# Late pieces of a second weight matrix: eight instead of six, in finer steps, and two groups' second layer moved into the third group

## The chip, the cores and the metric

The kernel runs on one core of one Trainium2 chip. What counts is device time in microseconds for one execution of the whole program. Three runs of the kernel before took 918.93, 920.24 and 922.5 us; their median is 920.24 us.

## The reference

Three layers follow each other: causal attention with a decay, a routed layer of experts of which each token uses one, and a dense two-layer network. The change lies in the weights of the last of them and touches the time around it.

```python
x = _moe_ref(x=attention_out, **moe_kwargs)      # 2304 tokens, 512 wide
...
def _moe2_ref(x, w_in, w_out, alpha):
    h = x @ w_in                                 # 512 -> 2048
    g = np.maximum(h, 0.0) + alpha * np.minimum(h, 0.0)
    return (g @ w_out).astype(np.float32)        # 2048 -> 512
```

The caller hands over `w_in` and `w_out` as 64-bit floats.

## The kernel before

Every matrix product is made of 16-bit halves: a number is held as a high half and the rest as a low half, and three matmuls (high by high, high by low, low by high) stand for one. The weights come from memory in 64 bits, so a piece of 128 rows by 512 columns is first turned to 32 bits on DVE by five bit operations (`ffn_bits`, L1445 to L1462) and then split (`ffn_split`, L1465): ACT writes the high half (L1474), DVE subtracts it for the low half (L1475). There are 32 pieces: 16 of `w_in` (tile `wi`) and 16 of `w_out` (tiles `wo` and, for the late ones, `wob`).

*The stage of token blocks.* Some 20 blocks of 128 gathered tokens go through their expert's two layers: `hidden` (L1186, 24 matmuls for both halves of a block, then ACT and DVE make the halves `hs`), `hturn` (L1209, SP transposes them by DMA into `ht`), and `outer` (L1221, 24 matmuls that read `ht`, then ACT and DVE write `yr`, and GpSimd scatters it to `ys`). The loop over `s` issues `hidden` and `hturn` of block `s + 1` ahead of `outer` of block `s`; blocks are called by these numbers below. Between them stand steps of a list `work`: 26 pieces of the dense weights (`KH + 16 - LATE`) and, one after every third piece, 8 parts of the third expert's weights. A step (`convert`, L1515) does the bits of one entry, the split of the entry before, and fetches the entry four later into one of four buffers. For an expert part the first half of a step is the high half on ACT and the second the low half on DVE (`part_hi`, `part_lo`, L1490 and L1495). The steps are dealt out evenly over the loop, half before and half after `outer`:

```python
    per = len(work) / (NS - NX - 0.5)
        due += per / 2
        while at_[1] < min(due, len(work)):
            convert()
        outer(s, wsel(s)[1])
```

With `NS` 20 and `NX` 7 the divisor is 12.5. A fetch is issued by SP, in the order of the program, and so are the transposes.

*The dense layers.* Tokens come in five groups: group 0 of 256, groups 1 to 4 of 512. `ffn_in(j, m)` makes one of 16 tiles of the first layer for group `j`: 12 matmuls into one of four PSUM buffers (L1668), two DVE operations that read it (L1673, L1676), the high half `g` on ACT (L1680), the low half on GpSimd (L1681). `ffn_out(j, t)` makes the output of 128 tokens: 48 matmuls over all 16 `g` tiles of its group (L1690), a copy on ACT, a scatter on GpSimd. The pool of `g` has 26 buffers. The outputs of group `j - 1` follow inside group `j`, in group 1 after tile 7, later after tile 3 (L1730).

The 6 pieces that are left (`LATE`) are converted here: `late_step` (L1706) is called once ahead of the loop and at seven tiles, and does the split of one piece, the bits of the next and the fetch of the one after it. The order of all engines' instructions is that of the program, from the token blocks on.

Of the kernel before, what the change touches and what calls it, by code (L numbers as in the profile page):

```python
# [11 lines left out]
F16 = mybir.dt.float16  # L12
# [73 lines left out]
SI = 32.0  # L86
SO = 64.0
# [4 lines left out]
def kernel(  # L92
# [19 lines left out]
    N, DM = out.shape  # L112
    E, _, F = w1.shape
    DFF = w_in.shape[1]
    P = 128
# [3 lines left out]
    KH = DFF // P  # L119
# [20 lines left out]
    G0 = 256  # L140
# [1272 lines left out]
    cvp = mid.enter_context(tc.tile_pool(name="cvp", bufs=2))  # L1413
    wst[0] = mid.enter_context(tc.tile_pool(name="wst3", bufs=4))
    with_w = ctx.enter_context(tc.tile_pool(name="wffn", bufs=1, side="right"))
    LATE = 6
    wi = with_w.tile([P, 2, KD, DFF], F16, name="wi")
    wo = [with_w.tile([P, 2, KH - LATE, DM], F16, name="wo")]
    x2a = with_w.tile([P, 2, KD, G0], F16, name="x2a")
# [42 lines left out]
        )  # L1462
        return tk

    def ffn_split(g, tk):  # L1465
        if g < 16:
            dk, cg = divmod(g, 4)
            cs_ = slice(cg * 512, cg * 512 + 512)
            dst, sc = wi, SI
        else:  # L1470
            y, dk = divmod(g - 16, KH - LATE)
            cs_ = slice(0, DM)
            dst, sc = wo[y], SO
        nc.scalar.activation(out=dst[:, 0, dk, cs_], in_=tk, func=AF.Copy, scale=sc)  # L1474
        nc.vector.scalar_tensor_tensor(  # L1475
            out=dst[:, 1, dk, cs_], in0=tk, scalar=sc, in1=dst[:, 0, dk, cs_], op0=ALU.mult, op1=ALU.subtract
        )


    ex2 = nc.sync.value_load(i8[0:1, 2:3], min_val=0, max_val=E - 1)  # L1480
# [18 lines left out]

    PS = (KH + 16 - LATE) // (KD + KF // 2)  # L1500
    work = []
    for g in range(KH + 16 - LATE):
        work.append((lambda g=g: ffn_fetch(g), lambda t, g=g: ffn_bits(g, t), lambda t, g=g: ffn_split(g, t)))
        if g % PS == 0 and g // PS < KD + KF // 2:
            y = g // PS
# [135 lines left out]
    gp = ctx.enter_context(tc.tile_pool(name="gp", bufs=26))  # L1641
# [9 lines left out]
    groups = [(0, G0)] + [(t, min(512, N - t)) for t in range(G0, N, 512)]  # L1651
# [10 lines left out]
    def ffn_in(j, m):  # L1662
        n = groups[j][1]
        x2 = x2s[j]
        hps = ps_a.tile([P, 512], F32, tag="a", name="a")
        for kk in range(KD):
            for y, (l, mm) in enumerate(((0, 0), (0, 1), (1, 0))):
                nc.tensor.matmul(  # L1668
                    hps[:, 0:n], lhsT=wi[:, mm, kk, m * P:(m + 1) * P], rhs=x2[:, l, kk, 0:n],
                    start=(kk == 0 and y == 0), stop=(kk == KD - 1 and y == 2),  # L1670
                )
        t = fp.tile([P, 512], F32, tag="t", name="t")
        nc.vector.tensor_scalar(  # L1673
            out=t[:, 0:n], in0=hps[:, 0:n], scalar1=0.0, scalar2=al[:, m:m + 1], op0=ALU.min, op1=ALU.mult
        )
        nc.vector.scalar_tensor_tensor(  # L1676
            out=t[:, 0:n], in0=hps[:, 0:n], scalar=0.0, in1=t[:, 0:n], op0=ALU.max, op1=ALU.add
        )
        g = gp.tile([P, 2, 512], F16, tag="g", name="g")
        nc.scalar.activation(out=g[:, 0, 0:n], in_=t[:, 0:n], func=AF.Copy)  # L1680
        nc.gpsimd.tensor_tensor(out=g[:, 1, 0:n], in0=t[:, 0:n], in1=g[:, 0, 0:n], op=ALU.subtract)  # L1681
        gts[j, m] = g

    def ffn_out(j, t):
        t0, n = groups[j]
        ops = ps_o.tile([P, DM], F32, tag="o", name="o")
        for m in range(KH):
            g = gts[j, m]
            for y, (l, mm) in enumerate(((0, 0), (0, 1), (1, 0))):
                nc.tensor.matmul(  # L1690
                    ops, lhsT=g[:, l, t * P:(t + 1) * P], rhs=wo[m // (KH - LATE)][:, mm, m % (KH - LATE), :],
                    start=(m == 0 and y == 0), stop=(m == KH - 1 and y == 2),
                )
        ob = fp.tile([P, DM], F32, tag="ob", name="ob")
        nc.scalar.activation(out=ob, in_=ops, func=AF.Copy, scale=1.0 / (SY * SI * SO))  # L1695
        ti = t0 // P + t
        nc.gpsimd.indirect_dma_start(  # L1697
            out=out[:, :], out_offset=IndirectOffsetOnAxis(ap=tka[:, ti:ti + 1], axis=0), in_=ob,
            in_offset=None, bounds_check=N - 1, oob_is_err=False,
        )  # L1700
# [2 lines left out]
    lraw = []  # L1703
    lbits = []

    def late_step():  # L1706
        if lbits:
            g, tk = lbits.pop(0)
            ffn_split(g, tk)
        if lraw:  # L1710
            g, raw = lraw.pop(0)
            lbits.append((g, ffn_bits(g, raw)))
        if late:
            g = late.pop(0)
            lraw.append((g, ffn_fetch(g)))

    x2s[0] = x2a
    order2 = ExitStack()
    order2.enter_context(tc.manual_schedule(engines=
# [3 lines left out]
    for j in range(len(groups)):  # L1723
        if j + 1 < len(groups):
            load_x2(j + 1)
        for m in range(KH):
            ffn_in(j, m)
            if (j, m) in ((0, 5), (0, 10), (0, 15), (1, 1), (1, 3), (1, 5), (1, 6)):
                late_step()
            if m == (7 if j == 1 else 3) and j > 0:  # L1730
                for t in range(groups[j - 1][1] // P):
                    ffn_out(j - 1, t)
    for t in range(groups[-1][1] // P):
        ffn_out(len(groups) - 1, t)
    order2.close()
# [30 lines left out]
```

## Time and profile before

| | us |
|---|---|
| median of three runs | 920.24 |
| profiled execution, its own time | 921.76 |
| its span, first to last instruction | 920.0 |
| TensorE busy | 802.4 (87%) |
| DVE busy | 503.6 (55%) |
| ACT busy | 320.8 (35%) |
| GpSimd busy | 287.1 (31%) |

The mean granted clock of TensorE is 0.950 of full speed. Busy time is an average over stages: the 87% holds stretches without a gap and stretches that wait, so the views by stretch and by time are the ones to read. Matmuls overlap, and the duration of one (379 ns) is longer than the distance between two. An idle time in square brackets is what the engine stood before that instruction, with what ended it.

### The profile page before, as it was taken

To read this page: it belongs to the slowest core of one execution; us is meant where nothing else is said; L and a number is where in the kernel's file an instruction comes from. 1 tells how busy PE (TensorE), PEld (TensorE's weight loads), DVE (VectorE), ACT (ScalarE), POOL (GpSimd) and SP (SyncE) were. 2 spreads that over 40 slices of the span, in tenths; PEclk is the share of its full clock that TensorE was granted. 3 is DMA by queue.
4 is the path that set the end of the run, shared out by engine and by line. 5 is a ranking of instruction groups with operands and counts; after the bars stand their busy time and mean duration, and the time that the engine had idled before them with its cause. 6 is when DMAs were issued, how large, how long until landed. Compare 5 with 4: busy or idle time off the path is not lost. (4 is left out here: it accounts for less than half of the span.)

```text
span 920.0 us, 15632 instructions
## 1 busy us (share of the span) xinstructions
PE 802.4 (87%) x5562; PEld 448.4 (49%) x5565; DVE 503.6 (55%) x1244; ACT 320.8 (35%) x630; POOL 287.1 (31%) x347
## 2 busy tenths in 40 slices
PE   3887759667988786989998899999999999999995
PEld 2676747554766332434443384444444444444442
DVE  6887859695785253668886768542035005302400
ACT  5786648574665122423232222121012002101200
POOL 4444344342435224421321133232034104302400
PEclk9998889887999897999999999999999999999998
DMA  7979999999852897999999354002002000000000
GB/s 151 167 134 183 160 130 175 183 195 167 133 77 60 137 145 193 257 267 223 244 233 240 92 120 114 12 12 58 24 12 46 12 35 1 1 24 23 1 24 23
DMA packets 226632, 103.17 MB, mean 112 GB/s; under 512 B 192843, under 2 KB 213944, under 8 KB 226554
## 3 DMA queue, kind: packets, MB, share of 16 engines
q1 hardware_dynamic: 221018, 87.29, 51.8%
q0 software_dynamic: 5536, 14.86, 4.7%
q8 instruction: 46, 0.75, 0.4%
q14 instruction: 32, 0.26, 0.1%
HBM read 49.06 MB, written 15.59 MB: 70 GB/s over the span
## 5 line engine op out<-in xcount | busy, mean ns | idle before, releaser
L1668 PE MATMUL a<-x,wi 128*128 128x512 f16 x768 | 168.2, 382 | 0.0
L1673 DVE TENSOR_SCALAR t<-a,al 128x512 f32<-128x512 f32 (+1 forms) x80 | 55.6, 695 | 203.7 <-PE a L1668 203.7
L1668 PEld LDWEIGHTS <-wi 128*128 128x128 f16 x960 | 95.2, 99 | 100.0 <-issue 7.5
L1690 PEld LDWEIGHTS <-g 128*128 128x128 f16 x864 | 84.5, 98 | 103.7 <-POOL g L1681 1.2
L1681 POOL TENSOR_TENSOR g<-t,g 128x512 f16<-128x512 f32 (+1 forms) x80 | 84.7, 1059 | 128.4 <-ACT g L1680 126.7
L1231 PE MATMUL y<-wcc,ht 128*128 (+1 forms) x456 | 108.3, 394 | 15.3 <-DMA ht<-hs 15.1
L1690 PE MATMUL o<-wo,g 128*128 128x512 f16 x540 | 119.5, 379 | 0.0
L1196 PE MATMUL h<-wcc,xgt 128*128 (+1 forms) x456 | 106.7, 390 | 11.3 <-DMA xgt<-xg 10.9
L1680 ACT ACTIVATE g<-t 128x512 f16<-128x512 f32 (+1 forms) x80 | 46.9, 587 | 163.9 <-DVE t L1676 163.9
L662 PE MATMUL pt<-identf,t 128*128 128x128 f32 x384 | 66.1, 298 | 32.3 <-DVE p L678 14.3
L650 ACT ACTIVATE t<-e,nm 128x512 f32<-128x512 f32 (+2 forms) x144 | 81.4, 603 | 18.5 <-DVE e L627 13.7
L1231 PEld LDWEIGHTS <-ht 128*128 128x128 f16 x480 | 47.7, 100 | 78.3 <-DMA ht<-hs 21.2
L1196 PEld LDWEIGHTS <-xgt 128*128 128x128 f16 x480 | 47.6, 100 | 69.5 <-DMA xgt<-xg 11.5
L678 DVE SCALAR_TENSOR_TENSOR p<-pt,p 128x512 f16<-128x512 f32 x96 | 65.4, 682 | 23.8 <-ACT p L671 23.3
L1690 PE MATMUL o<-wob,g 128*128 128x512 f16 x324 | 73.2, 379 | 1.5 <-DVE wob L1475 0.9
L1695 ACT ACTIVATE ob<-o 128x512 f32<-128x512 f32 x18 | 10.7, 596 | 158.2 <-PE o L1690 158.2
L627 DVE TENSOR_SCALAR_CACHE_REDUCE e<-s 128x512 f32<-128x512 f32 (+3 forms) x128 | 58.0, 480 | 13.1 <-PE s L580 13.1
L1697 POOL DMA_INDIRECT out_dram<-ob,tka x18 | 17.6, 978 | 151.3 <-ACT ob L1695 151.2
L662 PEld LDWEIGHTS pt<-identf,t 128*128 128x128 f32 x384 | 43.7, 150 | 36.2 <-ACT t L650 20.2
L671 ACT ACTIVATE p<-pt 128x512 f16<-128x512 f32 x96 | 56.2, 586 | 12.4 <-PE pt L662 12.1
L1676 DVE SCALAR_TENSOR_TENSOR t<-a,t 128x512 f32<-128x512 f32 (+1 forms) x80 | 51.0, 638 | 2.8
L579 PE MATMUL s<-yw,wcc 128*128 128x256 f16 (+1 forms) x192 | 47.4, 273 | 4.0 <-DMA yw<-wcc 4.0
(307 smaller groups left out, 1097.7 us busy)
## 6 DMA issues: line engine op xcount, KB each, us to landing
raw<-in_moe_w_in_dram SPq DMA_DIRECT2D x16, 512.0 KB, 7.1
raw<-in_moe_w_out_dram SPq DMA_DIRECT2D x16, 512.0 KB, 3.8
yw<-wcc SPq DMA_DIRECT2D x14, 320.0 KB, 5.0
kn<-in_k_dram SPq DMA_DIRECT2D x16, 256.0 KB, 4.3
qn<-in_q_dram SPq DMA_DIRECT2D x32, 128.0 KB, 4.4
vn<-in_v_dram SPq DMA_DIRECT2D x16, 256.0 KB, 4.0
xs<-nat SPq DMA_DIRECT2D x16, 256.0 KB, 7.1
ht<-hs SPq DMA_TRANSPOSE x40, 4.9
```

The lines of the kernel that those rows point to most:

```text
L627: nc.vector.tensor_scalar(out=e[:, c0:c0 + w], in0=ps[:, c0:c0 + w], scalar1=-1.0 / 8.0, scalar2=3.0e38, op0=ALU.mult, op1=ALU.min, accum_ ...
L650: nc.scalar.activation(out=natural(t[:, c0:c0 + w]), in_=halves(e[:, c0:c0 + w]), func=AF.Exp, scale=-1.0, bias=nm[:, y:y + 1])
L662: nc.tensor.transpose(pt[:, c * P:(c + 1) * P], e[:, c * P:(c + 1) * P], identf)
L671: nc.scalar.activation(out=p[:, 0, 0:512], in_=U[u][0], func=AF.Copy, scale=SP)
L678: nc.vector.scalar_tensor_tensor(out=p[:, 1, 0:512], in0=U[u][0], scalar=SP, in1=p[:, 0, 0:512], op0=ALU.mult, op1=ALU.subtract)
L1196: nc.tensor.matmul(hps, lhsT=xgt[:, kk, l, :], rhs=m1(m, kk, cs_), start=(kk == 0 and y == 0), stop=(kk == KD - 1 and y == 2),)
L1231: nc.tensor.matmul(yps, lhsT=ht[:, kk // (KF // 2), l, kk % (KF // 2), :], rhs=m2(m, kk), start=(kk == 0 and y == 0), stop=(kk == KF - 1 a ...
L1668: nc.tensor.matmul(hps[:, 0:n], lhsT=wi[:, mm, kk, m * P:(m + 1) * P], rhs=x2[:, l, kk, 0:n], start=(kk == 0 and y == 0), stop=(kk == KD - ...
L1673: nc.vector.tensor_scalar(out=t[:, 0:n], in0=hps[:, 0:n], scalar1=0.0, scalar2=al[:, m:m + 1], op0=ALU.min, op1=ALU.mult)
L1676: nc.vector.scalar_tensor_tensor(out=t[:, 0:n], in0=hps[:, 0:n], scalar=0.0, in1=t[:, 0:n], op0=ALU.max, op1=ALU.add)
L1681: nc.gpsimd.tensor_tensor(out=g[:, 1, 0:n], in0=t[:, 0:n], in1=g[:, 0, 0:n], op=ALU.subtract)
L1690: nc.tensor.matmul(ops, lhsT=g[:, l, t * P:(t + 1) * P], rhs=wo[m // (KH - LATE)][:, mm, m % (KH - LATE), :], start=(m == 0 and y == 0), s ...
```

## The change

`LATE` becomes 8, so that `wo` holds 8 pieces and `wob` 8, and the list `work` has 24 pieces and 8 parts. The late step is cut finer: the high half stands in one step and the low half in the next, so that a piece goes through four steps (fetch, bits, high half, low half), and within a step the low half of the oldest piece comes first. There are ten calls in the loop instead of seven, the last two in group 2. The outputs of groups 0 and 1 both come after tile 7 of group 2; group 0's `g` tiles get 16 smaller buffers of their own.

```diff
@@ -1413,7 +1413,7 @@
     cvp = mid.enter_context(tc.tile_pool(name="cvp", bufs=2))
     wst[0] = mid.enter_context(tc.tile_pool(name="wst3", bufs=4))
     with_w = ctx.enter_context(tc.tile_pool(name="wffn", bufs=1, side="right"))
-    LATE = 6
+    LATE = 8
     wi = with_w.tile([P, 2, KD, DFF], F16, name="wi")
     wo = [with_w.tile([P, 2, KH - LATE, DM], F16, name="wo")]
     x2a = with_w.tile([P, 2, KD, G0], F16, name="x2a")
@@ -1462,19 +1462,26 @@
         )
         return tk
 
-    def ffn_split(g, tk):
+    def ffn_place(g):
         if g < 16:
             dk, cg = divmod(g, 4)
-            cs_ = slice(cg * 512, cg * 512 + 512)
-            dst, sc = wi, SI
-        else:
-            y, dk = divmod(g - 16, KH - LATE)
-            cs_ = slice(0, DM)
-            dst, sc = wo[y], SO
+            return wi, SI, dk, slice(cg * 512, cg * 512 + 512)
+        y, dk = (0, g - 16) if g - 16 < KH - LATE else (1, g - 16 - (KH - LATE))
+        return wo[y], SO, dk, slice(0, DM)
+
+    def ffn_high(g, tk):
+        dst, sc, dk, cs_ = ffn_place(g)
         nc.scalar.activation(out=dst[:, 0, dk, cs_], in_=tk, func=AF.Copy, scale=sc)
+
+    def ffn_low(g, tk):
+        dst, sc, dk, cs_ = ffn_place(g)
         nc.vector.scalar_tensor_tensor(
             out=dst[:, 1, dk, cs_], in0=tk, scalar=sc, in1=dst[:, 0, dk, cs_], op0=ALU.mult, op1=ALU.subtract
         )
+
+    def ffn_split(g, tk):
+        ffn_high(g, tk)
+        ffn_low(g, tk)
 
 
     ex2 = nc.sync.value_load(i8[0:1, 2:3], min_val=0, max_val=E - 1)
@@ -1676,7 +1683,10 @@
         nc.vector.scalar_tensor_tensor(
             out=t[:, 0:n], in0=hps[:, 0:n], scalar=0.0, in1=t[:, 0:n], op0=ALU.max, op1=ALU.add
         )
-        g = gp.tile([P, 2, 512], F16, tag="g", name="g")
+        if j == 0:
+            g = gp.tile([P, 2, G0], F16, tag="g0", name="g0", bufs=KH)
+        else:
+            g = gp.tile([P, 2, 512], F16, tag="g", name="g")
         nc.scalar.activation(out=g[:, 0, 0:n], in_=t[:, 0:n], func=AF.Copy)
         nc.gpsimd.tensor_tensor(out=g[:, 1, 0:n], in0=t[:, 0:n], in1=g[:, 0, 0:n], op=ALU.subtract)
         gts[j, m] = g
@@ -1686,9 +1696,10 @@
         ops = ps_o.tile([P, DM], F32, tag="o", name="o")
         for m in range(KH):
             g = gts[j, m]
+            wm, mo = (wo[0], m) if m < KH - LATE else (wo[1], m - (KH - LATE))
             for y, (l, mm) in enumerate(((0, 0), (0, 1), (1, 0))):
                 nc.tensor.matmul(
-                    ops, lhsT=g[:, l, t * P:(t + 1) * P], rhs=wo[m // (KH - LATE)][:, mm, m % (KH - LATE), :],
+                    ops, lhsT=g[:, l, t * P:(t + 1) * P], rhs=wm[:, mm, mo, :],
                     start=(m == 0 and y == 0), stop=(m == KH - 1 and y == 2),
                 )
         ob = fp.tile([P, DM], F32, tag="ob", name="ob")
@@ -1703,10 +1714,16 @@
     lraw = []
     lbits = []
 
+    lhalf = []
+
     def late_step():
+
+        if lhalf:
+            ffn_low(*lhalf.pop(0))
         if lbits:
             g, tk = lbits.pop(0)
-            ffn_split(g, tk)
+            ffn_high(g, tk)
+            lhalf.append((g, tk))
         if lraw:
             g, raw = lraw.pop(0)
             lbits.append((g, ffn_bits(g, raw)))
@@ -1714,6 +1731,8 @@
             g = late.pop(0)
             lraw.append((g, ffn_fetch(g)))
 
+
+    LSTEPS = ((0, 5), (0, 11), (1, 0), (1, 3), (1, 6), (1, 9), (1, 12), (1, 15), (2, 2), (2, 5))
     x2s[0] = x2a
     order2 = ExitStack()
     order2.enter_context(tc.manual_schedule(engines=
@@ -1725,11 +1744,12 @@
             load_x2(j + 1)
         for m in range(KH):
             ffn_in(j, m)
-            if (j, m) in ((0, 5), (0, 10), (0, 15), (1, 1), (1, 3), (1, 5), (1, 6)):
+            if (j, m) in LSTEPS:
                 late_step()
-            if m == (7 if j == 1 else 3) and j > 0:
-                for t in range(groups[j - 1][1] // P):
-                    ffn_out(j - 1, t)
+            if m == (7 if j == 2 else 3) and j > 1:
+                for i in (0, 1) if j == 2 else (j - 1,):
+                    for t in range(groups[i][1] // P):
+                        ffn_out(i, t)
     for t in range(groups[-1][1] // P):
         ffn_out(len(groups) - 1, t)
     order2.close()
```

What moves on the engines is shown at three places. First DVE in group 0, around the second late step in the loop (`t` is a tile's result, `ta` and `tb` the bit tiles, `wob` the late weights); before, after tile 10:

```order
L1673 TENSOR_SCALAR t<-a,al 128x256
L1676 SCALAR_TENSOR_TENSOR t<-a,t 128x256
L1475 SCALAR_TENSOR_TENSOR wob<-ta,wob 128x512
L1451 TENSOR_SCALAR ta<-raw 128x512
L1452 TENSOR_SCALAR ta<-ta 128x512
L1454 TENSOR_SCALAR tb<-ta 128x512
L1457 SCALAR_TENSOR_TENSOR tb<-raw,tb 128x512
L1460 SCALAR_TENSOR_TENSOR ta<-raw,tb 128x512
L1673 TENSOR_SCALAR t<-a,al 128x256
L1676 SCALAR_TENSOR_TENSOR t<-a,t 128x256
```

and now, after tile 11:

```order
L1680 TENSOR_SCALAR t<-a,al 128x256
L1683 SCALAR_TENSOR_TENSOR t<-a,t 128x256
L1451 TENSOR_SCALAR ta<-raw 128x512
L1452 TENSOR_SCALAR ta<-ta 128x512
L1454 TENSOR_SCALAR tb<-ta 128x512
L1457 SCALAR_TENSOR_TENSOR tb<-raw,tb 128x512
L1460 SCALAR_TENSOR_TENSOR ta<-raw,tb 128x512
L1680 TENSOR_SCALAR t<-a,al 128x256
L1683 SCALAR_TENSOR_TENSOR t<-a,t 128x256
```

The low half left this step; the five bit operations stay, one tile later.

Next DVE in the token blocks, from the first conversion that follows `yr` of block 8 to `hs` of block 10. Before (the bits of the first conversion and `yr` stand just ahead):

```order
L1475 SCALAR_TENSOR_TENSOR wi<-ta,wi 128x512
L1451 TENSOR_SCALAR ta<-raw 128x512
L1452 TENSOR_SCALAR ta<-ta 128x512
L1454 TENSOR_SCALAR tb<-ta 128x512
L1457 SCALAR_TENSOR_TENSOR tb<-raw,tb 128x512
L1460 SCALAR_TENSOR_TENSOR ta<-raw,tb 128x512
L1475 SCALAR_TENSOR_TENSOR wi<-ta,wi 128x512
L1204 SCALAR_TENSOR_TENSOR hs<-h,hs 128x512 x2
```

and now, from `yr` of block 8:

```order
L1244 SCALAR_TENSOR_TENSOR yr<-y,gs,yr 128x512
L1451 TENSOR_SCALAR ta<-raw 128x512
L1452 TENSOR_SCALAR ta<-ta 128x512
L1454 TENSOR_SCALAR tb<-ta 128x512
L1457 SCALAR_TENSOR_TENSOR tb<-raw,tb 128x512
L1460 SCALAR_TENSOR_TENSOR ta<-raw,tb 128x512
L1478 SCALAR_TENSOR_TENSOR wi<-ta,wi 128x512
L1204 SCALAR_TENSOR_TENSOR hs<-h,hs 128x512 x2
```

One conversion of five bit operations and a low half left this stretch.

Last SP's queue in the dense layers, where `raw` is a late fetch and `x` a group's tokens. Before:

```order
L1440 DMA raw<-in_moe_w_out_dram 128x1024
L1423 DMA_TRANSPOSE x_7726<-ys 128x8x512
L1428 DMA tka<-ys 128x4x1
L1440 DMA raw<-in_moe_w_out_dram 128x1024 x3
L1423 DMA_TRANSPOSE x_8064<-ys 128x8x512
L1428 DMA tka<-ys 128x4x1
L1440 DMA raw<-in_moe_w_out_dram 128x1024 x2
L1423 DMA_TRANSPOSE x_8512<-ys 128x8x512
L1428 DMA tka<-ys 128x4x1
L1423 DMA_TRANSPOSE x_9035<-ys 128x8x512
L1428 DMA tka<-ys 128x4x1
```

and now:

```order
L1440 DMA raw<-in_moe_w_out_dram 128x1024
L1423 DMA_TRANSPOSE x_7704<-ys 128x8x512
L1428 DMA tka<-ys 128x4x1
L1440 DMA raw<-in_moe_w_out_dram 128x1024 x2
L1423 DMA_TRANSPOSE x_8030<-ys 128x8x512
L1428 DMA tka<-ys 128x4x1
L1440 DMA raw<-in_moe_w_out_dram 128x1024 x5
L1423 DMA_TRANSPOSE x_8401<-ys 128x8x512
L1428 DMA tka<-ys 128x4x1
L1423 DMA_TRANSPOSE x_9035<-ys 128x8x512
L1428 DMA tka<-ys 128x4x1
```

Group 2's tokens are loaded after two fetches in group 0 rather than three, and five fetches stand ahead of group 3's tokens.

## Rows read from the trace of the kernel before

**Rows 1.** Stretches, TensorE: start:end and length, busy (instructions), granted clock, DMA share, GB/s.

```profile
376.00:527.00 151.00, 139.06 (x632) 0.99 0.92 226
600.00:900.00 300.00, 300.00 (x1392) 1.00 0.07 21
```

**Rows 2.** TensorE's waits, 376 to 527 us: us in total, times, longest.

```profile
PE y L1231 <- DMA ht<-hs: 11.7, 7, 2.6
```

**Rows 3.** Order of time, TensorE, outer products: start, us, instruction, [idle before and releaser].

```profile
411.22 6.83 PE L1231 MATMUL y<-wcc,ht 128*128 x24 [2.58 <-DMA ht<-hs]
...
425.04 5.34 PE L1231 MATMUL y<-wcc,ht 128*128 x24 [1.82 <-DMA ht<-hs]
...
447.62 5.34 PE L1231 MATMUL y<-wcc,ht 128*128 x24 [1.70 <-DMA ht<-hs]
...
479.66 5.34 PE L1231 MATMUL y<-wcc,ht 128*128 x24 [0.62 <-DMA ht<-hs]
...
491.91 0.38 PE L1231 MATMUL y<-wcc,ht 128*128 x1 [1.73 <-DMA ht<-hs]
...
521.37 5.36 PE L1231 MATMUL y<-w2x,ht 128*128 128x512 f16 x24 [1.98 <-DMA ht<-hs]
```

**Rows 4.** Order of time, DVE and SP's queue around block 9's transposes.

```profile
402.60 1.22 DVE L1497 SCALAR_TENSOR_TENSOR w1x<-wst__6087,w1x 128x1024 f16<-128x1024 f32 x1
...
404.48 5.09 SPq L1217 DMA_TRANSPOSE ht<-hs  x2
```

**Rows 5.** Groups of DVE instructions, 376 to 527 us: busy, mean ns, idle before.

```profile
L1204 DVE SCALAR_TENSOR_TENSOR hs<-h,hs 128x512 f16<-128x512 f32 x26 | 17.2, 684 | 12.4 <-ACT hs L1203 12.4
...
L1475 DVE SCALAR_TENSOR_TENSOR wi<-ta,wi 128x512 f16<-128x512 f32 x16 | 10.9, 683 | 1.4 <-ACT wi L1474 1.4
...
L1244 DVE SCALAR_TENSOR_TENSOR yr<-y,gs,yr 128x512 f16<-128x512 f32 x13 | 9.7, 746 | 12.3 <-ACT yr L1243 12.3
```

**Rows 6.** Order of time, 530 to 620 us: around the late steps.

```profile
548.61 0.74 DVE L1475 SCALAR_TENSOR_TENSOR wob<-ta,wob 128x512 f16<-128x512 f32 x1 [1.00 <-ACT wob L1474]
549.27 0.42 DVE L1451 TENSOR_SCALAR ta<-raw 128x512 uint32<-128x512 uint32 x1
...
551.99 0.48 DVE L1673 TENSOR_SCALAR t<-a,al 128x256 f32<-128x256 f32 x1
...
552.84 0.47 DVE L1673 TENSOR_SCALAR t<-a,al 128x256 f32<-128x256 f32 x1
...
552.98 1.58 PE L1668 MATMUL a<-x2a,wi 128*128 128x256 f16 x12 [1.95 <-DVE t L1676]
...
560.70 0.74 DVE L1673 TENSOR_SCALAR t<-a,al 128x512 f32<-128x512 f32 x1
...
562.08 0.74 DVE L1673 TENSOR_SCALAR t<-a,al 128x512 f32<-128x512 f32 x1
...
562.86 0.69 DVE L1676 SCALAR_TENSOR_TENSOR t<-a,t 128x512 f32<-128x512 f32 x1
562.90 1.16 POOL L1681 TENSOR_TENSOR g<-t,g 128x512 f16<-128x512 f32 x1 [5.39 <-ACT g L1680]
...
587.17 0.38 PE L1690 MATMUL o<-wob,g 128*128 128x512 f16 x1 [0.61 <-ACT wob L1474]
...
588.43 0.59 PE L1690 MATMUL o<-wob,g 128*128 128x512 f16 x2 [0.88 <-DVE wob L1475]
```

**Rows 7.** Chain of work that ended last: start, us, engine.

```profile
599.38 31.08 PE a L1668 x144
```

**Rows 8.** Stretches of 4 us, TensorE, columns as in rows 1.

```profile
554.00:558.00 4.00, 4.00 (x15) 0.57 1.17 285
...
586.00:590.00 4.00, 2.51 (x12) 1.00 0.00 0
```

**Rows 9.** Instructions of the conversion tiles: ns least/median/most, first and last start.

```profile
L1454 DVE TENSOR_SCALAR tb<-ta x32: 426/427/778, 380.9 to 582.7; 128x512 uint32<-128x512 uint32 x32
...
L1475 DVE SCALAR_TENSOR_TENSOR wob<-ta,wob x6: 741/1224/1230, 548.6 to 587.1; 128x512 f16<-128x512 f32 x6
```

## The prediction

> **What bounds the kernel now.** I read the stretches of engine time first, then TensorE's waits, then the order of time around each wait.
>
> From 600 to 900 us TensorE is busy without a break at full clock [rows 1]. Nothing the change does there can save time, unless it opens a gap. From 376 to 527 us, the stage of token blocks, TensorE is busy for 139.06 of 151 us [rows 1], and its one named wait is for the transposed hidden block `ht`: 11.7 us in all [rows 2]. Two kinds of wait can be told apart in order of time [rows 3]. The outer products at 411.22, 447.62 and 479.66 (blocks 9, 12, 15) come after a half block whose last conversion step is an expert part. SP's next fetch then needs a buffer that only that part's low half frees, so the transposes queue behind it: the low half at 402.60, the transposes from 404.48 [rows 4]. Those at 425.04, 491.91 and 521.37 (blocks 10, 16, 19) come after a block with three bit conversions on DVE.
>
> Between 529 and 600 us lie three losses around the late pieces. DVE stands 1.00 us before the low half at 548.61, because it follows the high half in the same step, and then runs five bit operations (549.27 to 551.99); four PSUM buffers fill and TensorE stands 1.95 us [rows 6]. From 554 to 558 the granted clock is 0.57 [rows 8], a mix of the levels 1.2 and 2.4 GHz, so 4 x 0.43 = 1.72 us are lost. At 587 TensorE stands 0.61 and 0.88 us for the last late piece [rows 6]; the clock stays at 1.00 there [rows 8]. Sum: 1.95 + 1.72 + 1.49 = **5.16 us**.
>
> **The change, part by part.**
>
> *The second step of group 0* now holds only bits. Before, DVE gave TensorE nothing from about 547.5 (the end of its work on the eleventh tile) to 551.99, some 4.5 us. Now it is 2.72 us (549.27 to 551.99 [rows 6]), or 3.07 if one operation is stretched as the longest 778 ns against 427 [rows 9]. A group-0 tile takes TensorE 1.30 us (half of 31.08/12 = 2.59 [rows 7]), and three free buffers cover 3.9 us. DVE needs 0.85 us per tile there (551.99 to 552.84 [rows 6]), so the six tiles between steps give back 6 x 0.45 = 2.7 us. No stall; the 1.95 and the 1.72 go.
>
> *The steps in group 1* come every three tiles: DVE spends 3 x 1.38 (560.70 to 562.08 [rows 6]) + 2.72 bits + 0.68 low [rows 5] = 7.54 us against TensorE's 3 x 2.59 = 7.77. High halves run on ACT a step ahead, so the 1.00 us wait is gone. If the low half takes 1.23 and one bit operation 0.78 [rows 9], it is 8.44: 0.67 lag per step, 4.0 over six steps. The cover is three buffers, 7.77, less one step's 4.3: 3.5 us. So the worst by these rows is half a microsecond of stall, perhaps with one more 1.72 of clock, and I take none. Here the cover is nearly used up: if DVE is slower than that, its tiles are late next.
>
> *The two moved pieces* add to this stage two fetches, ten bit operations, two high and two low halves. The DVE part is in the sums above, the high halves go to ACT beside one operation per tile. SP now issues eight fetches; each waits for the bits of the piece two earlier, and behind the last five stands only group 3's load, which TensorE reads after the 62 us of output tiles.
>
> *Second layer later.* TensorE runs group 1 whole and half of group 2 (24 tiles, 24 x 2.59 = 62 us) before the first late piece is read; that is at about 552 + 62 + 24 matmuls x 0.216 = 619. The last low half comes after the sixth tile of group 2, at about 610. The 1.49 goes. Six output tiles in a row follow instead of two and four; matmuls and scatters are the same in number. The separate smaller buffers for group 0 hold its results longer: with 16 of group 1 and 8 of group 2, 24 of 26 buffers are in use. Cost nothing.
>
> *The stage of token blocks* loses two of 26 pieces: 2 x (2.72 + 0.68) = 6.8 us of DVE, and two fetches on SP. A block costs TensorE 48 matmuls of 0.216 (31.08/144 [rows 7]), 10.36 us. Three bit conversions in a block make DVE 3 x 2.72 + 2 x 0.68 + 1.22 [rows 4] + 0.75 + 2 x 0.68 [rows 5] = 12.9; with two it is 9.5. By the rule in the code, 34 steps become 32 over 12.5 blocks: three-bit blocks fall from four to two (blocks 13 and 16; hidden blocks 15 and 18 follow them), part-last half blocks from four to three (before blocks 9, 14, 17). Block 9 keeps its 2.58. For 14 and 17 I take the mean of 1.70 and 0.62, 1.16 each. Of the first three three-bit blocks two cost 1.82 and 1.73 and one nothing: 1.18 each for the two left. Block 19's 1.98 goes: between hs of 18 and of 19 DVE now has one bit conversion where it had three. The 1.3 us of 11.7 that lies outside the six rows I leave. Sum 2.58 + 2.32 + 2.36 + 1.3 = 8.5, a gain of **3.2 us**. Bounds: all waits but block 9's vanish (gain 9.1); the five marked blocks all wait 2.58, 12.9 in all (loss 1.2).
>
> Total 5.16 + 3.2 = 8.4 us. The profiled execution took 921.76, so 913.4; it lies 1.5 above the median of the runs, 920.24. Against the median: **911.9 us**.
>
> **The rivals.**
>
> *The waits in the token blocks only move* (TensorE, no longer late, meets the next transpose early). For: waits there also follow slow transposes, not DVE alone. Against: the three-bit blocks. 920.24 - 5.16 = 915.1.
>
> *The split does not do what it says:* in group 0 the bits are the stall, not the wait for ACT, and 1.95 + 1.72 stay. Against: 2.72 is below the cover of 3.9. 920.24 - 1.49 - 3.2 = 915.5.
>
> *Slower: GpSimd holds DVE up in group 1.* The wob low halves took 741 to 1230 ns [rows 9] where the same operation takes 683 [rows 5]; GpSimd's subtraction of g lasts 1.16 us [rows 6], once per tile, and the late steps now run amid it instead of after a wait. If each subtraction holds DVE for its whole length, three tiles cost 7.54 + 3 x 1.16 = 11.0 us against 7.77: 3.2 lag, 19.4 over six steps, less 3.5 cover: 15.9 of stall, with 1.72 of clock. 920.24 - 5.16 + 17.6 - 3.2 = 929.5. It decides from about 1.8 us of lag per step, where stall and clock eat the 8.4. Against: the stretch seen is 0.55 us, not 1.16, and the tile operation at 562.86 keeps its 0.69 with the subtraction at 562.90 beside it [rows 6]. The Trainium skill has this as a rule ("SBUF — State Buffer", section "Who interferes with whom"): a DVE instruction with two SBUF inputs and a GpSimd instruction that reads SBUF use one shared read interface, and the second to start waits for the whole of the first. By that rule it would come out as in this rival; the trace agrees that there is a hold-up, but with about half that size.
>
> **How the numbers follow.** Forecast 0.64, moving waits 0.22, split without effect 0.09, slower 0.05. A measurement of this kernel tells 0.5% from no change, 4.6 us: faster is below 915.6. The forecast counts as faster; the two cases near 915 count by a little over half (0.13 and 0.05): faster 0.82, same 0.13, slower 0.05. The range: from 906.5 (the gain of 9.1 nearly whole, with 5.16) to 917, which takes in both cases near 915 with half the bound of 1.2 and one half-microsecond stall with its clock.
>
> **What would show it.** Right: no TensorE wait for `t` or `wob`, no clock below 1.00 between 535 and 600, DVE without waits for ACT at wob's low half, the six output tiles in one block of 62 us, and `ht` waits near 8.5 us with none at block 10 or 19. Wrong: a TensorE wait for `t` in group 1 or 2, low halves over 1.23 us, or `ht` waits of 11 us or more.

## The result, and the profile after

The changed kernel took 909.13 us (median of four runs, 903.85 to 917.96), the kernel before 919.59 on the same chip (four runs, 918.5 to 922.5). The ratio is 0.989, with an interval of 0.985 to 0.993: faster by 6.8 to 13.6 us. Ratios and intervals, here and below, leave out executions in the chip's second, slower state, so a ratio is not quite that of the two medians. The forecast was 911.9, 8.3 us below the kernel before. The total came out near; two of its terms did not, and they erred in opposite directions.

The page's first lines of the changed kernel, the share of each engine (its profiled execution took 907.73 us):

```profile
span 905.6 us, 15603 instructions
## 1 busy us (share of the span) xinstructions
PE 796.8 (88%) x5565; PEld 446.1 (49%) x5565; DVE 511.5 (56%) x1244; ACT 320.6 (35%) x630; POOL 291.5 (32%) x347
```

DVE is busy for 7.9 us more than the 503.6 before (4.4 more in the repetition below), though the same pieces are converted. That is the first sign that some operations became longer. TensorE's waits from 360 us to the end of the changed kernel (total, times, longest):

```profile
PE y L1231 <- DMA ht<-hs: 6.8, 2, 3.8
PE a L1675 <- DVEq L1564: 2.8, 1, 2.8
PE a L1675 <- DVE t L1683: 2.7, 4, 1.0
```

The waits for `ht` fell from 11.7 us in 7 to 6.8 in 2 [rows 2]. The waits for `wob` are gone. The wait of 2.8 ahead of the dense layers is as it was. The waits for `t`, which were to go, are four now. In order of time on TensorE, the places of these waits in the token blocks and group 0's start:

```profile
407.44 7.03 PE L1231 MATMUL y<-wcc,ht 128*128 x24 [3.82 <-DMA ht<-hs]
...
495.41 5.35 PE L1231 MATMUL y<-wcc,ht 128*128 x24 [2.99 <-DMA ht<-hs]
...
510.96 5.34 PE L1231 MATMUL y<-w2x,ht 128*128 128x512 f16 x24
...
519.13 11.08 PE L1675 MATMUL a<-x2a,wi 128*128 128x256 f16 x100 [2.83 <-DVEq L1564]
```

Only blocks 9 (407.44) and 17 (495.41) wait, both after a half block that ends with an expert part; block 14, the third such, does not. Block 19 (510.96) waits for nothing, where it stood 1.98 us [rows 3]. The dense layers of the changed kernel, TensorE, DVE and GpSimd in order of time:

```profile
540.67 36.42 PE L1675 MATMUL a<-x,wi 128*128 128x512 f16 x168 [0.42 <-DVE t L1683]
...
553.35 1.15 DVE L1478 SCALAR_TENSOR_TENSOR wob<-ta,wob 128x512 f16<-128x512 f32 x1
...
561.63 0.69 DVE L1683 SCALAR_TENSOR_TENSOR t<-a,t 128x512 f32<-128x512 f32 x1
561.68 1.16 POOL L1691 TENSOR_TENSOR g<-t,g 128x512 f16<-128x512 f32 x1 [0.23 <-ACT g L1690]
562.24 1.15 DVE L1478 SCALAR_TENSOR_TENSOR wob<-ta,wob 128x512 f16<-128x512 f32 x1
...
563.06 1.34 POOL L1691 TENSOR_TENSOR g<-t,g 128x512 f16<-128x512 f32 x1 [0.22 <-ACT g L1690]
563.42 1.27 DVE L1451 TENSOR_SCALAR ta<-raw 128x512 uint32<-128x512 uint32 x1
564.72 0.43 DVE L1452 TENSOR_SCALAR ta<-ta 128x512 f32<-128x512 f32 x1
...
577.40 7.93 PE L1675 MATMUL a<-x,wi 128*128 128x512 f16 x36 [0.31 <-DVE t L1683]
586.29 7.93 PE L1675 MATMUL a<-x,wi 128*128 128x512 f16 x36 [0.97 <-DVE t L1683]
```

From low half to low half, 553.35 to 562.24, three tiles and a step last 8.89 us on DVE; TensorE takes 7.77 for them. So DVE falls back by 1.12 per step, until from 577 us TensorE waits once in every step. Where the 8.89 comes from stands in the rows between. The low half starts while one subtraction runs and takes 1.15 where 0.68 is its length alone [rows 5]; the first bit operation starts while the next subtraction runs and takes 1.27 where the second one takes 0.43. These two add 0.47 and 0.84. The tile `wob` tells the first for all eight pieces (shortest, median and longest in ns), and that none waits for ACT any more, since no idle time is listed for L1478:

```profile
L1478 DVE SCALAR_TENSOR_TENSOR wob<-ta,wob x8: 680/1146/1149, 544.9 to 603.0; 128x512 f16<-128x512 f32 x8
```

TensorE's clock in two stretches of the changed kernel (start and end, length, busy us and count of PE, PEld, DVE, ACT and POOL, granted clock, DMA share, GB/s):

```profile
519.13:523.13 4.00, 4.00 (x37) 3.58 (x38) 1.82 (x4) 0.00 (x0) 0.51 (x1) 1.00 0.55 163
538.00:542.00 4.00, 3.58 (x28) 2.48 (x27) 3.83 (x9) 0.83 (x2) 0.68 (x2) 1.00 0.35 95
```

The 0.57 at group 0's late pieces [rows 8] is gone. So is a loss that the prediction had overlooked: in the kernel before the clock was low over the first 4 us of group 0 as well.

```profile
529.55:533.55 4.00, 4.00 (x23) 3.00 (x24) 0.91 (x2) 0.42 (x1) 0.69 (x2) 0.59 0.22 41
```

In the changed kernel's execution it was 1.00 there, by nothing that the change does, as the repetition below shows.

For the comparison of stages I cut every trace at three points: the start of block 6's outer product, the end of block 19's, and group 0's first matmul. "Blocks" is the first stretch, "dense" runs from the third point to the span's end; between them lie 2.82 to 2.83 us in every trace. "Clock" is what low stretches of the dense layers cost: their length times one less the granted clock. All times are us; the spans are read to a tenth, so the last digit of "dense" is loose.

| profiled execution | block 6 starts | blocks | of it `ht` waits | dense | waits for `t`, `wob` | clock |
|---|---|---|---|---|---|---|
| before | 377.4 | 149.3 | 11.7 | 390.45 | 3.4 | 1.64 + 1.72 |
| changed | 372.4 | 143.9 | 6.8 | 386.47 | 2.7 | 0 |
| changed again | 387.0 | 145.5 | 8.0 | 387.93 | 2.6 | 1.52 |
| six late pieces | 384.3 | 146.5 | 9.2 | 385.93 | 0.7 | 1.72 |
| split in one step | 392.8 | 142.7 | 5.6 | 391.01 | 6.8 | 0 |
| subtraction on ACT | 387.7 | 144.0 | 6.9 | 383.81 | 0.4 | 0 |
| five buffers | 384.0 | 140.2 | 2.6 | 386.46 | 2.6 | 0 |
| order alone | 391.3 | 151.2 | 12.5 | 392.35 | 8.4 | 0 |
| split alone | 384.4 | 149.9 | 12.2 | 386.23 | 2.4 | 0 |
| outputs back | 383.6 | 144.9 | 6.5 | 395.43 | 11.2 | 0 |
| steps every four | 377.2 | 144.4 | 7.5 | 383.81 | 0.4 | 0 |
| four and five | 391.2 | 141.7 | 4.4 | 383.77 | 0.4 | 0 |

Two things make the table usable. Dense less its waits and its clock losses is 383.4 to 384.2 in all twelve, so waits and clock are all that differs there. And the start of block 6, ahead of which no kernel here differs, lies anywhere between 372 and 393 us: a total, of one profile or of a few runs, carries that scatter, and these stages do not. The blocks hold a low stretch of the clock too, which the last column leaves out: 1.7 us of cost in each execution, and 3.4 in three of them (order alone, outputs back, four and five). Of the 14.4 us between the first two spans, 5.0 come from the stages ahead of block 6 and are not the change's.

### The profile page after: what moved, and what is told of

The parts are those of the page before. It is cut to its first block, busy times and chain, and to the rows that moved or that the text cites. A ratio compares the mean times of both kernels' runs of the same rounds, so it can differ in the third digit from the quotient of the medians.

```text
span 905.6 us, 15603 instructions
## 1 busy us (share of the span) xinstructions
PE 796.8 (88%) x5565; PEld 446.1 (49%) x5565; DVE 511.5 (56%) x1244; ACT 320.6 (35%) x630; POOL 291.5 (32%) x347
## 5 line engine op out<-in xcount | busy, mean ns | idle before, releaser
L1690 ACT ACTIVATE g<-t 128x512 f16<-128x512 f32 (+1 forms) x80 | 46.7, 586 | 148.0 <-DVE t L1683 141.7
L1701 PE MATMUL o<-wo,g 128*128 128x512 f16 x432 | 96.2, 379 | 0.0
L1701 PE MATMUL o<-wob,g 128*128 128x512 f16 x432 | 96.2, 379 | 0.0
```

The source lines that it names most:

```text
L1701: nc.tensor.matmul(ops, lhsT=g[:, l, t * P:(t + 1) * P], rhs=wm[:, mm, mo, :], start=(m == 0 and y == 0), stop=(m == KH - 1 and y == 2),)
```

## The experiments

These theories were set against each other: after the change DVE is held by GpSimd's subtraction for part of each step (the slower rival's mechanism, with a smaller price), the split of the step is what keeps DVE from standing still, and two pieces less are what shortens the token blocks. The runs came in three lots, each on one chip with the kernel before beside it. Diffs are against the changed kernel unless said.

**Six late pieces.** The order and the finer steps stay, two pieces go back to the token blocks.

```diff
-    LATE = 8
+    LATE = 6
```

> Only LATE goes back to 6; four steps per piece, ten places and the later outputs stay. Theory (the token blocks gain because two pieces leave them): TensorE's waits for ht between outer 6 and outer 19 are back near the 11.7 us of before, against 6.8 in the changed kernel, and that stretch lasts 149 us, against 143.9. In the dense layers six pieces make two steps fewer, so DVE's lag of 1.1 us per step in group 1 gathers over four steps instead of six: waits for t under 1 us instead of 2.7. Rival (the difference in the blocks is only the scatter of DMA times): the stretch stays near 144 us.

Measured 923.19 against 930.85, ratio 0.993 (0.990 to 0.996). Dense waits are 0.7 us, as expected; blocks are 146.5 us, half way between the two kernels instead of at the old value. A single profile of the blocks scatters: the four kernels with 26 pieces there (before, this, order alone, split alone) have 149.3, 146.5, 151.2 and 149.9, mean 149.2; the six with 24 pieces and four buffers have 142.7 to 145.5, mean 144.2. So the two pieces are worth some 5.0 us in the blocks (4.8 without the low clock there), a figure that one pair of profiles could not give. Its sign is safe, its size only roughly known: the shortest of the four (146.5) and the longest of the six (145.5) are 1.0 us apart.

**The split in one step again,** with eight pieces in the new places.

```diff
-            ffn_high(g, tk)
-            lhalf.append((g, tk))
+            ffn_split(g, tk)
```

> High and low half stand in one step again; eight pieces, the ten places and the later outputs stay. Theory of the prediction (the wait for ACT ahead of the low half made group 0's stall): DVE waits some 1.0 to 1.2 us ahead of each of the eight low halves, the step after tile 11 of group 0 blocks DVE for 4.5 us again, and TensorE stands 1.5 to 2 us there, with or without a clock loss of 1.7. Rival (while DVE waits for ACT, GpSimd's subtraction gets done, so what is gained in waiting is paid in hold-up): steps in group 1 cost the same 8.9 us per three tiles as in the changed kernel or less, and the dense layers take as long, within 1 us, but for group 0.

Measured 926.93, ratio 0.996 (0.992 to 1.000). The waits of TensorE from 536 us on, and two low halves in order of time on DVE:

```profile
PE a L1675 <- DVE t L1683: 6.8, 6, 1.5
```

```profile
576.30 1.23 DVE L1478 SCALAR_TENSOR_TENSOR wob<-ta,wob 128x512 f16<-128x512 f32 x1 [1.21 <-ACT wob L1474]
577.46 0.41 DVE L1451 TENSOR_SCALAR ta<-raw 128x512 uint32<-128x512 uint32 x1
...
585.61 1.23 DVE L1478 SCALAR_TENSOR_TENSOR wob<-ta,wob 128x512 f16<-128x512 f32 x1 [1.21 <-ACT wob L1474]
```

DVE stands 1.21 us for the high half in each step, three tiles and a step are 9.31 us, and the waits grow from 2.7 to 6.8; the longest, 1.55, is back in group 0. The split is worth 4.1 us of wait with eight pieces: the rival in which it does nothing is out. But that rival named a true part: after the wait the first bit operation meets no subtraction and takes 0.41, not 1.27. So of the 1.21 us that the split saves in a step of group 1, 0.86 are paid back there, and the step becomes shorter by 0.42 alone (9.31 against 8.89).

**The subtraction off GpSimd.** For group 1 alone ACT writes a copy of `t` into the low half of `g`. The kernel leaves out that group's subtraction, so its second layer is computed from another low half than the reference's; the run is for the times of DVE.

```diff
-        nc.gpsimd.tensor_tensor(out=g[:, 1, 0:n], in0=t[:, 0:n], in1=g[:, 0, 0:n], op=ALU.subtract)
+        if j == 1:
+            nc.scalar.activation(out=g[:, 1, 0:n], in_=t[:, 0:n], func=AF.Copy)
+        else:
+            nc.gpsimd.tensor_tensor(out=g[:, 1, 0:n], in0=t[:, 0:n], in1=g[:, 0, 0:n], op=ALU.subtract)
```

> In group 1 the low half of g is not made by GpSimd's subtraction; ACT writes a copy of t in its place, so the second layer of group 1 is computed with another low half. Theory (GpSimd's subtraction holds DVE up once in each late step of group 1): the low half takes 0.68 us and not 1.15, the first bit operation 0.42 and not 1.27, three tiles with a step take 7.6 us and not 8.9, below TensorE's 7.77, and the waits for t in groups 1 and 2 fall from 2.3 us to under 0.3. Rival (the late steps are slow for another reason, PSUM or the queue): lengths and waits stay.

Measured 919.67 against 930.85, ratio 0.987 (0.983 to 0.990). The start of a step in order of time on DVE, and TensorE's waits for `t` from 386 us on:

```profile
568.04 0.68 DVE L1478 SCALAR_TENSOR_TENSOR wob<-ta,wob 128x512 f16<-128x512 f32 x1
568.75 0.43 DVE L1451 TENSOR_SCALAR ta<-raw 128x512 uint32<-128x512 uint32 x1
```

```profile
PE a L1675 <- DVE t L1683: 0.4, 1, 0.4
```

Both operations have their length alone, the waits in group 1 are gone (the 0.4 left is group 0's), and dense falls to 383.81. This shows the cause: the subtraction holds DVE up, by 1.3 us in a step.

**Five buffers** for the pieces on their way.

```diff
-    wst[0] = mid.enter_context(tc.tile_pool(name="wst3", bufs=4))
+    wst[0] = mid.enter_context(tc.tile_pool(name="wst3", bufs=5))
```

> The fetch buffers of the token blocks are five instead of four; the fetch stays four entries ahead, so none waits for an expert part's low half. Theory (a part that ends a half block holds SP's queue, and the transposes behind it): ht of block 9 and of block 17 is issued some 4 us earlier after its hs, and of the waits of 3.8 and 3.0 us at outer 9 and outer 17 at most 1.5 us is left in all; the stretch from outer 6 to outer 19 is 139 to 141 us. Rival (the transposes themselves are slow in a crowded DMA, 6 us and more): the waits stay within 1.5 us of 6.8.

Measured 915.82, ratio 0.985 (0.982 to 0.989); blocks 140.2 us, `ht` waits 2.6. What changed is seen at block 17. In the changed kernel, DVE and SP in order of time:

```profile
483.49 0.69 DVE L1204 SCALAR_TENSOR_TENSOR hs<-h,hs 128x512 f16<-128x512 f32 x1 [0.50 <-ACT hs L1203]
...
486.25 0.69 DVE L1460 SCALAR_TENSOR_TENSOR ta<-raw,tb 128x512 uint32<-128x512 uint32 x1
...
486.87 1.22 DVE L1504 SCALAR_TENSOR_TENSOR w2x<-wst__6954,w2x 128x1024 f16<-128x1024 f32 x1
486.98 0.39 SPq L192 DMA_DIRECT2D wst__7109<-in_moe_w_dram  x1
...
488.76 4.27 SPq L1217 DMA_TRANSPOSE ht<-hs  x2
```

The halves `hs` are done at 484.18, but SP is held at a fetch ahead of the transposes (486.98), and the transposes start at 488.76, 4.6 us late. What held the fetch is the next piece's bits: it goes out when the last bit operation ends (486.95), while the part's low half runs on until 488.09. SP's own wait, from 480 to 488 us:

```profile
SPq L192 <- DVE ta L1460: 5.3, 1, 5.3
```

With five buffers:

```profile
493.86 0.69 DVE L1204 SCALAR_TENSOR_TENSOR hs<-h,hs 128x512 f16<-128x512 f32 x1 [1.00 <-ACT hs L1203]
494.56 3.18 SPq L1217 DMA_TRANSPOSE ht<-hs  x2
497.24 1.22 DVE L1504 SCALAR_TENSOR_TENSOR w2x<-wst__6954,w2x 128x1024 f16<-128x1024 f32 x1
```

They start at the end of `hs`, ahead of bits and low half. So the prediction read the queue rightly in this: SP waits for a buffer, and the transposes stand behind it. What frees the buffer it had wrong. Of the 2.6 us that are left, 2.2 stand at block 14, which waits in no profile with 24 pieces and four buffers.

**The changed kernel again.**

> The changed kernel once more, unaltered. What comes ahead of outer 6 is the same program in both kernels, and took 377.4 us before and 372.4 in the changed kernel's profile. Theory (these 5 us are scatter of the early stages, no part of the change): outer 6 starts anywhere between 372 and 393 us, while the token blocks from outer 6 on repeat within 2 us of 143.9 and the dense layers within 1 us of 386.5. Rival (the change moves the early stages too): outer 6 starts earlier than in every run of a kernel with LATE 6.

Measured 926.53 against 933.38, ratio 0.996 (0.991 to 1.000). Block 6 starts at 387.0 us, among those of the four kernels with 26 pieces there (377.4 to 391.3), so nothing shows that the change moves the stages ahead. The blocks are 1.6 us longer than in the first execution and the dense layers 1.5; the latter is the clock over group 0's first 4 us, which this time was low:

```profile
535.37:539.37 4.00, 4.00 (x24) 3.02 (x25) 0.91 (x2) 0.00 (x0) 0.50 (x1) 0.62 0.50 159
```

The interval allows a gain of up to 8.3 us, with 4.2 in its middle; that of the first comparison 6.8 to 13.6, with 10.2 in its middle. Both hold between 6.8 and 8.3.

**The order alone,** against the kernel before: the outputs of groups 0 and 1 in group 2 (the small buffers with them), six pieces in the old places.

```diff
-            if m == (7 if j == 1 else 3) and j > 0:
-                for t in range(groups[j - 1][1] // P):
-                    ffn_out(j - 1, t)
+            if m == (7 if j == 2 else 3) and j > 1:
+                for i in (0, 1) if j == 2 else (j - 1,):
+                    for t in range(groups[i][1] // P):
+                        ffn_out(i, t)
```

> The kernel before with one part of the change: the outputs of groups 0 and 1 come after tile 7 of group 2 (with the small buffers for group 0); six late pieces, whole split, seven places as before. Theory (only the wait for wob hangs on the order): the 1.5 us of waits for wob go, the 1.95 us for t in group 0 stay with their clock loss, and the dense layers take 388.5 to 389.5 us against 390.45. Rival (the order brings a cost of its own, through six outputs in a row or the buffers): the dense layers take 390 us or more.

Measured 934.57, ratio 1.004 (0.999 to 1.008). TensorE in order of time:

```profile
567.00 1.47 PE L1668 MATMUL a<-x2a,wi 128*128 128x256 f16 x12 [1.94 <-DVE t L1676]
...
592.10 5.34 PE L1668 MATMUL a<-x,wi 128*128 128x512 f16 x24 [2.58 <-DVE t L1676]
600.03 2.75 PE L1668 MATMUL a<-x,wi 128*128 128x512 f16 x12 [2.59 <-DVE t L1676]
```

The expectation failed. No wait for `wob` is left, but 8.4 us of waits for `t` stand in their place, 6.4 of them in group 1. There the old steps come every one or two tiles; two tiles and a step are 7.9 us on DVE against 5.2 on TensorE. In the kernel before, the two output tiles of group 0, 20.7 us of matmuls that ask nothing of DVE, stood right behind those steps, after tile 7, and let DVE catch up before the PSUM buffers were used up; here the two longest waits are behind tiles 7 and 9. The moved outputs had been hiding a lag.

**The split alone:** outputs in place as before, six pieces, the finer steps in places of their own.

```diff
-    LATE = 8
+    LATE = 6
...
-    LSTEPS = ((0, 5), (0, 11), (1, 0), (1, 3), (1, 6), (1, 9), (1, 12), (1, 15), (2, 2), (2, 5))
+    LSTEPS = ((0, 5), (0, 10), (0, 15), (1, 1), (1, 3), (1, 5), (1, 6), (1, 7))
...
-            if m == (7 if j == 2 else 3) and j > 1:
-                for i in (0, 1) if j == 2 else (j - 1,):
-                    for t in range(groups[i][1] // P):
-                        ffn_out(i, t)
+            if m == (7 if j == 1 else 3) and j > 0:
+                for t in range(groups[j - 1][1] // P):
+                    ffn_out(j - 1, t)
```

> Six late pieces in four steps each, with the outputs where they were before, so the steps stand as before plus one more at tile 7 of group 1. Theory (the steps need the room that the later outputs give): DVE no longer waits for ACT, group 0's stall falls to under 0.7 us, but steps every two tiles of group 1 cost 2.8 + 4.7 us against TensorE's 5.2, so waits of 1 to 4 us for t or wob come up ahead of the outputs: dense layers 387 to 392 us. Rival (the split alone is the gain): no wait over 0.7 us and 386 us or less.

Measured 927.33 against 933.38, ratio 0.996 (0.991 to 1.001). TensorE's waits from 536 us on:

```profile
PE o L1701 <- DVE wob L1478: 1.6, 2, 1.0
PE a L1675 <- DVE t L1683: 0.9, 1, 0.9
```

Dense is 386.23 us, as good as the whole change's 386.47. That lies between the expectations: waits of 2.4 us, as the theory had them, and a stage just below its range. In the dense layers the order brings nothing by itself; what it gives is room for two more pieces there.

**Eight pieces with the outputs back** in their old place, the steps dense enough to be in time for them.

```diff
-    LSTEPS = ((0, 5), (0, 11), (1, 0), (1, 3), (1, 6), (1, 9), (1, 12), (1, 15), (2, 2), (2, 5))
+    LSTEPS = ((0, 3), (0, 6), (0, 9), (0, 12), (0, 15), (1, 1), (1, 2), (1, 4), (1, 5), (1, 6))
...
-            if m == (7 if j == 2 else 3) and j > 1:
-                for i in (0, 1) if j == 2 else (j - 1,):
+            if m == (7 if j == 1 else 3) and j > 0:
+                for i in (j - 1,):
```

> Eight late pieces in four steps each, but the outputs of group 0 after tile 7 of group 1 as before, so that the ten steps are packed into the first 23 tiles. Theory (the later outputs are what makes room for eight pieces): the 24 tiles ahead of the outputs give DVE 16 x 0.85 + 8 x 1.38 us of tiles and eight times 3.4 to 4.7 us of conversion, 52 to 62 us against TensorE's 41; less some 8 us of buffers and the 10 us of matmuls ahead of the last late piece, TensorE waits 4 to 13 us for t and wob, and the dense layers take 388 to 396 us. Rival (the steps fit anyway, the order is free to choose): waits under 3 us as in the changed kernel, 386.5 us. The token blocks take 143 to 145 us in either case.

Measured 925.4 against 925.66, ratio 1.003 (0.998 to 1.008). From 530 us on TensorE waits:

```profile
PE a L1675 <- DVE t L1683: 11.2, 6, 2.9
```

That is the price of the two pieces without the order: 8.5 us more of waits than with it, which eats the 5.0 of the blocks.

**Steps every four tiles** in place of every three.

```diff
-    LSTEPS = ((0, 5), (0, 11), (1, 0), (1, 3), (1, 6), (1, 9), (1, 12), (1, 15), (2, 2), (2, 5))
+    LSTEPS = ((0, 5), (0, 11), (1, 0), (1, 4), (1, 8), (1, 12), (2, 0), (2, 3), (2, 5), (2, 7))
```

> The changed kernel with the late steps at every fourth tile of group 1 alone; four fetch buffers. Theory: dense layers 383.8 us apart from clock losses, with at most 0.4 us of waits for t as with both changes together; token blocks 143 to 145.5 us as in the changed kernel, with waits at outer 9 and outer 17. Rival (the room comes from the five buffers): waits for t near 2.7 us.

Measured 909.3 (two runs, hence the wide interval) against 925.66, ratio 0.982 (0.970 to 0.994). Dense is 383.81 us: four tiles give TensorE 10.4 us for a step, and DVE keeps up. With four buffers as before, the rival that the room comes from five is out.

**Steps every four and five buffers together.** Both diffs above.

> The changed kernel with five fetch buffers in the token blocks and the late steps at every fourth tile of group 1 (the last at tile 7 of group 2). Theory: four tiles with a step cost DVE 8.9 + 1.4 = 10.3 us against TensorE's 10.4, so no lag gathers and the waits for t fall from 2.7 to under 0.8 us; the blocks take about 140 us as with five buffers alone; together the dense layers take 384 to 385 us and the run is 5 to 6 us below the changed kernel on the same chip. Rival (the lag is not what causes the waits, or the last low half is now too late for the second layer): waits for t stay over 2 us, or waits for wob come up.

Measured 915.24 against 926.53 for the changed kernel on the same chip and 933.38 before; ratio to before 0.980 (0.970 to 0.990). The start of two steps in order of time on DVE:

```profile
571.88 0.68 DVE L1478 SCALAR_TENSOR_TENSOR wob<-ta,wob 128x512 f16<-128x512 f32 x1
572.60 0.43 DVE L1451 TENSOR_SCALAR ta<-raw 128x512 uint32<-128x512 uint32 x1
573.06 1.26 DVE L1452 TENSOR_SCALAR ta<-ta 128x512 f32<-128x512 f32 x1
...
582.24 0.68 DVE L1478 SCALAR_TENSOR_TENSOR wob<-ta,wob 128x512 f16<-128x512 f32 x1
```

A DVE that is not late starts its low half when no subtraction runs, and the low half loses its stretch of 0.47. The other stretch stays: the second bit operation takes 1.26 here, as the first did in the changed kernel. What keeps DVE in time is the fourth tile. Blocks and dense together are 8.0 us below the changed kernel's repetition, of which 1.5 are the low clock at the repetition's group 0; what the 11.3 of the runs hold beyond that lies outside these two stages or in the scatter of executions. One thing did not fit: with five buffers block 9 still waited here,

```profile
PE y L1231 <- DMA ht<-hs: 4.4, 1, 4.4
```

while in the run with five buffers alone it waited 0.4. Its transposes were issued at 417.5 us, and TensorE could read `ht` at 426.8. Why it took so long is open.

## Why the prediction was right or wrong

**The total** was near in part by luck, because two errors offset. By the table, blocks gained 5.0 us (means) against 3.2 forecast. Dense went from 390.45 to 386.47, or, with the low clock at group 0's start taken out of every execution that had it, from 388.8 to 386.4 (the changed kernel twice): 2.4 against 5.16 forecast. Together 7.4 us, where 8.4 was forecast and the two comparisons leave 6.8 to 8.3. The profiled 907.73 lies lower than that, for 5.0 us of scatter ahead of block 6; for the other three runs of the first comparison no trace tells.

**The second step of group 0:** right. Its wait of 1.95 and the clock of 0.57 after it went. A wait of 0.42 stands at 540.67 in their place. Two bit operations were stretched there, by 0.69 together, where the prediction allowed for one:

```profile
536.28 0.72 DVE L1451 TENSOR_SCALAR ta<-raw 128x512 uint32<-128x512 uint32 x1
537.03 0.82 DVE L1452 TENSOR_SCALAR ta<-ta 128x512 f32<-128x512 f32 x1
```

Whether the 1.72 of clock is always lost without the change is not settled: the order alone had the same wait, 1.94, and the clock stayed at 1.00.

**The steps in group 1:** this is the step that failed. It set 7.54 us for three tiles, 8.44 at worst, and took no stall. Measured: 8.89, with 2.2 us of stall (the other 0.42 of the 2.7 is group 0's); a wait for `t` in group 1 or 2 was among the signs of being wrong. The tiles and the other four bit operations were as priced; the low half cost 0.47 more and the first bit operation 0.84 more, each because a subtraction of GpSimd was running beside it. The worst case had the low half right (1.23) but took 0.35 for the bits because the longest of [rows 9], which is of another of the five operations, shows no more. The cover did what was said of it: the lag of 1.12 per step was swallowed for three steps and most of the fourth, and the "three buffers less one step" ran out at 577 us.

**The slower rival** had the right mechanism and the wrong count. It charged three whole subtractions per step, 3.5 us; two are met per step, each for what is left of it, 1.3 together. The lag of 1.12 stayed below the 1.8 at which it was to decide (1.7, when that sum is done again). The tile operations, with one input in PSUM, met subtractions without growing: the one at 561.63 kept its 0.69 beside the subtraction of 561.68. The bit operation that started at 563.42 ended at 564.69, 0.29 after the subtraction (563.06, 1.34 long), and so did little before that one's end. The Trainium skill says of GpSimd and a DVE operation in a two-port mode that the one that issued first keeps the shared pair of ports for its whole instruction and that the other blocks fully ("SBUF — State Buffer", section "Who interferes with whom"); it lists tensor_scalar among the operations that can enter such a mode. The trace agrees as to the whole length; it does not show the mode. I had applied the rule to operations with two SBUF inputs only, and the larger share, 0.84, fell on one with a single input.

**Second layer later, "the 1.49 goes":** the waits for `wob` did go, and no buffer of `g` held anyone up. But "cost nothing" was wrong. The order alone shows 8.4 us of new waits, because the output tiles had covered DVE's late steps. In the whole change 2.7 of waits are left. Wider steps and the split do that together: with the wider steps and the split undone they are 6.8, and no run widens the steps alone with six pieces.

**High halves a step ahead:** right. DVE waits for ACT ahead of no low half of `wob`, and putting the halves together costs 4.1 us.

**The token blocks:** the mechanism was right but for one reading, the sizes were not. The reading is that only a part's low half frees the buffer of SP's next fetch. In the kernel before, too, the fetch ahead of block 9's transposes goes out while that low half [rows 4] still runs:

```profile
402.71 0.34 SPq L189 DMA_DIRECT2D wst__6244<-in_moe_w_dram  x1
```

It waits for the next piece's bits, of which the last ends at 402.68; they stand ahead of the low half on DVE. For the forecast this changes little, since both come in the same step. Blocks 9 and 17 wait, 10 and 19 do not, as forecast (in the repetition 10 waited 0.97). Block 17 took 2.99 (1.16 forecast) and 9 took 3.82 (2.58). Block 14 stood 0 us where 1.16 was charged, and the blocks after three bit conversions, 15 and 18, 0 us where 2.36 was; in the repetition 15 took 1.16 and 14 and 18 nothing. The 1.3 us that the prediction left outside its six rows were a wait of 1.21 at block 17, so that block had in effect two charges, 2.5 in all. So the three-bit term and block 14's were over-charged, and those of blocks 9 and 17 fell short; the split of the 5.0 over blocks differs from one execution to the next, and no run here tells why.

**The two rivals near 915:** neither. The waits in the blocks did not merely move, and the split counts.

## What to carry to other kernels

When steps of one engine are moved among another engine's steady work, price them with that work running beside: here an operation of 0.43 us cost 1.27, and the price alone decided between keeping up and falling back. Before moving a long stretch of matmuls away, ask which engine has been catching up under it; its lag shows only when the cover has gone. And where the stages ahead scatter by 20 us, compare the stage that was changed, from several executions, before believing a total.

## What the runs showed of the hardware

Two matters were not expected. GpSimd's subtraction pays as well: 1.34 us in place of 1.16 where it started before a stretched low half had ended (563.06, the low half's end being 563.39).

And the same gap ahead of group 0, 2.82 to 2.83 us in all twelve executions, was followed by a granted clock of 0.57 to 0.62 over 4 us, a mix of the levels 1.2 and 2.4 GHz, in three of them (before, six late pieces, changed again) and by 1.00 in nine. Likewise a wait of 1.95 was followed by 0.57 in the kernel before and one of 1.94 by 1.00 with the order alone. After the same gap the loss came in some executions and not in others, so the single profile of before, from which the prediction took its 1.72, cannot price it.
